# First layer of the last six units as seven block products, with the order from unit 5's second half on written anew

## The chip, the cores and the metric

One NeuronCore of a Trainium2 chip runs the kernel. The metric is device time in microseconds: the median of three runs of the kernel before is 290.37 us (290.33 to 292.88). In the profile PE is TensorE's matmuls, PEld its weight loads, DVE VectorE, ACT ScalarE, POOL GpSimd, SP the engine that issues most DMAs.

## What is computed

Attention in which a query sees only the keys of its own hash bucket (six sign bits of a projection), then a layer norm and a two-layer MLP with a residual.

```python
q_bits = (np.einsum('bhsd,dk->bhsk', q, proj) > 0)        # q, k, v: 4 x 8 x 768 x 64
k_bits = (np.einsum('bhsd,dk->bhsk', k, proj) > 0)        # bucket = the six bits as a number
scores = np.where(q_bucket == k_bucket, 0.125 * q @ k.T, -1e9)
attn = softmax(scores) @ v
x = attn.transpose(0, 2, 1, 3).reshape(4, 768, 512)
xn = (x - mu) / np.sqrt(var + 1e-06) * g_ln
out = x + np.maximum(xn @ w_ch1, 0.0) @ w_ch2             # 512 -> 2048 -> 512
```

## The kernel before

The work is cut into 12 units: unit u holds 256 of the 768 tokens of batch u // 3. Batches 0 to 3 are loaded, transposed and cast one after the other while earlier units compute. In a unit the eight heads form two groups g of four.

The program is one list of words, ORDER, in which each word is a function of the kernel, an engine (t TensorE, v VectorE, a ScalarE, p GpSimd, s SyncE) and its numbers. Each engine carries out its own words in the list's order; waits between engines come from the tiles that they share. Which buffer of a pool a tile gets is also written out, as one digit per tile in SLOTS.

The words of a unit, in the order of the data:

- `S.t.u.g.k` (L591): scores of 128 keys against 256 queries, four heads at once on four row strips: twelve matmuls of 256 columns. They go into tiles of the PSUM pool pp, three buffers of two banks.
- `E.a` (L608): the exp of one such tile, 128x1024, on ScalarE, into one of 15 SBUF buffers of pool E.
- `A.t` (L619): eight matmuls of 65 columns (v and a column of ones) into the accumulator acc, which also lives in pp.
- `na`, `nb`, `nc`, `ag`, `rs`, `ce` (L631 to L687): the accumulator is read, divided by its row sum, its mean and variance are taken, and the centred rows xc are written in bf16. `fl` (L690) is a DMA that writes them transposed into xnT.
- `F.t.u.p` (L710): the first layer, eight chunks p of 256 hidden columns: two blocks of 128, each of four matmuls over the 512 inputs, 256 token columns each, into one bank of the PSUM pool f, which has two. `R` (L718 on ScalarE, L720 on VectorE) reads a chunk once, with the relu, into hb.
- `ss` (L850), `P.t.u.1` to `P.t.u.7` (L865), `Y` (L870): the second layer by seven block products instead of eight (Winograd's form of Strassen's scheme). ss makes the block sums of hb, each P is eight matmuls of 256 columns into a bank of f, and Y adds the product to x. `O` (L882, L884) stores the unit.

So pool f carries the chunks F, the products P and a few small tiles, and pp carries the scores and acc. On TensorE the words S, A, F and P of neighbouring units stand mixed: at any time unit u's scores, unit u - 1's chunks or unit u - 2's products.

The functions `W1s`, `w1s`, `bs`, `M_`, `V_`, `U_`, `Q_`, `ru` (a first layer by seven products) stand in the code before too, but no word of the list before calls them, and WIDE is empty.

Of the kernel before, what the change touches and what calls it, by code (L numbers as in the profile page):

```python
# [64 lines left out]
A.t.4.0.0.2 F.t.2.0 A.t.4.0.1.0 A.t.4.0.1.1 na.v.4.0 F.t.2.4 E.a.4.1.0.0 E.a.4.1.0.2 R.a.2.0 R.v.2.4 ss.v.2.1  # L65
tu.v.2.1.0.1 S.t.5.0.0 N.a.5.0.0 S.t.5.0.1 E.a.5.0.0.1 S.t.5.0.2 P.t.2.2 Y.v.2.2 E.a.5.0.0.0 E.a.5.0.0.2
nb.v.4.0 fl.s.3.1 F.t.3.6 R.v.3.6 ss.v.2.2 P.t.2.1 Y.v.2.1 cv.v.2.0.2 S.t.4.1.3 S.t.4.1.4 N.a.4.1.1 S.t.4.1.5
mr.s.2.0.1 P.t.2.5 P.t.2.6 E.a.4.1.1.1 E.a.4.1.1.2 ss.v.2.4 Y.v.2.5 tu.v.2.1.0.0 A.t.4.1.0.2 P.t.2.3
E.a.4.1.1.0 nc.v.4.0 Y.v.2.6 A.t.4.1.1.2 Y.v.2.3 O.s.1.3 LX.s.3.0.1 LX.s.3.1.0 LX.s.3.1.1 mr.s.2.0.0
A.t.4.1.1.0 A.t.4.1.0.1 A.t.4.1.1.1 tu.v.2.1.1.0 ss.v.2.3 A.t.4.1.0.0 na.v.4.1 nb.v.4.1 LX.s.3.0.0 mr.s.2.0.2  # L70
F.t.3.3 nc.v.4.1 ag.v.4.0 P.t.2.7 S.t.5.0.3 R.a.3.3 N.a.5.0.1 S.t.5.0.4 S.t.5.0.5 ag.v.4.1 E.a.5.0.1.2 Y.v.2.7
E.a.5.0.1.1 CA.v.2.1.1 E.a.5.0.1.0 hm.t.2.1 bt.v.2.1 P.t.2.4 rs.p.4 Y.v.2.4 ce.v.4.0 F.t.3.4 S.t.5.1.0
tu.v.3.0.1.1 tu.v.3.0.1.3 CA.v.2.1.0 S.t.5.1.1 N.a.5.1.0 ce.v.4.1 R.a.3.4 S.t.5.1.2 su.v.2.0 E.a.5.1.0.1
F.t.3.0 mw.s.2.1 F.t.3.7 mr.s.2.0.3 O.s.1.0 A.t.5.0.0.0 tu.v.3.0.1.0 A.t.5.0.1.2 A.t.5.0.0.1 A.t.5.0.0.2
tu.v.3.0.1.2 R.a.3.0 F.t.3.2 mr.s.2.1.3 cv.a.2.0.0 R.a.3.7 E.a.5.1.0.0 R.a.3.2 A.t.5.0.1.0 A.t.5.0.1.1
tu.v.3.0.0.3 E.a.5.1.0.2 O.s.2.2 lv.s.2.4.2 na.v.5.0 O.s.2.0 tu.v.3.0.0.1 F.t.3.5 R.a.3.5 fl.s.4.1 F.t.3.1
R.v.3.1 mr.s.2.1.0 S.t.5.1.3 N.a.5.1.1 S.t.5.1.4 E.a.5.1.1.1 S.t.5.1.5 E.a.5.1.1.2 nb.v.5.0 P.t.3.2 ss.v.3.1
Y.v.3.2 P.t.3.1 P.t.3.5 S.t.6.0.0 E.a.5.1.1.0 CA.v.3.0.1 N.a.6.0.0 mr.s.2.1.1 lv.s.3.0.2 S.t.6.0.1 S.t.6.0.2
E.a.6.0.0.0 E.a.6.0.0.2 ss.v.3.2 Y.v.3.1 ss.v.3.4 Y.v.3.5 P.t.3.6 P.t.3.3 ss.v.3.3 nc.v.5.0 A.t.5.1.0.1
A.t.5.1.0.2 tu.v.3.0.0.2 A.t.5.1.0.0 Y.v.3.6 A.t.5.1.1.0 A.t.5.1.1.2 A.t.5.1.1.1 mr.s.2.1.2 na.v.5.1  # L80
E.a.6.0.0.1 fl.s.4.0 lv.s.2.4.3 P.t.3.7 tu.v.3.0.0.0 Y.v.3.3 nb.v.5.1 O.s.2.3 S.t.6.0.3 N.a.6.0.1 S.t.6.0.4
S.t.6.0.5 CA.a.3.0.0 Y.v.3.7 hm.t.3.0 bt.v.3.0 P.t.3.4 Y.v.3.4 lv.s.3.0.3 F.t.4.6 E.a.6.0.1.0 O.s.2.1
E.a.6.0.1.2 E.a.6.0.1.1 lv.s.3.0.1 nc.v.5.1 ag.v.5.1 ag.v.5.0 R.a.4.6 F.t.4.0 S.t.6.1.0 S.t.6.1.1 N.a.6.1.0
rs.p.5 S.t.6.1.2 R.v.4.0 ce.v.5.0 cv.a.2.4.2 F.t.4.7 E.a.6.1.0.0 cv.v.2.4.0 F.t.4.4 R.a.4.7 ce.v.5.1 on.p.2
fl.s.5.0 A.t.6.0.1.0 A.t.6.0.0.2 tu.v.3.1.0.1 E.a.6.1.0.1 E.a.6.1.0.2 A.t.6.0.1.2 lv.s.3.0.0 R.v.4.4 sp.t.2.0
# [36 lines left out]
R.v.8.7 rs.p.9 ce.v.9.0 A.t.10.0.0.0 A.t.10.0.0.2 A.t.10.0.1.2 A.t.10.0.1.1 F.t.8.5 R.a.8.5 ce.v.9.1 Y.v.7.4
F.t.8.0 O.s.7.2 na.v.10.0 R.v.8.0 S.t.10.1.3 fl.s.9.1 S.t.10.1.4 N.a.10.1.1 S.t.10.1.5 O.s.7.0 E.a.10.1.1.1
E.a.10.1.1.2 E.a.10.1.1.0 F.t.8.2 nb.v.10.0 R.v.8.2 F.t.8.3 R.a.8.3 F.t.8.4 R.v.8.4 S.t.11.0.0 N.a.11.0.0
S.t.11.0.1 S.t.11.0.2 F.t.8.1 E.a.11.0.0.0 R.v.8.1 P.t.8.2 O.s.7.3 Y.v.8.2 ss.v.8.1 E.a.11.0.0.2 fl.s.9.0
A.t.10.1.1.0 P.t.8.1 A.t.10.1.0.2 F.t.9.5 Y.v.8.1 A.t.10.1.1.2 A.t.10.1.0.1 A.t.10.1.0.0 A.t.10.1.1.1 ss.v.8.2
ss.v.8.4 R.a.9.5 E.a.11.0.0.1 P.t.8.6 na.v.10.1 nb.v.10.1 P.t.8.5 Y.v.8.5 S.t.11.0.3 ss.v.8.3 Y.v.8.6
# [19 lines left out]

TYPES = "222222333333333333333333"

WIDE = {}  # L150
SUMS = 12

SLOTS = dict(
# [15 lines left out]
    vnat="01010101",  # L169
    vsB="0101",  # L170
    vsum="000",
    x="012301230123",
    xnT="010101010101",
)

@with_exitstack
def kernel(
# [15 lines left out]
    nc = tc.nc  # L193
# [595 lines left out]
    def hq(u, t, i, h):  # L789
        return hb(u)[:, 8 * i + 4 * h : 8 * i + 4 * h + 4, P * t : P * t + P]  # L790
# [138 lines left out]
```

## Time and profile before

| | us |
|---|---|
| median of 3 runs | 290.37 |
| the profiled execution's own time | 290.62 |
| its span, first to last instruction | 288.7 |
| PE busy | 280.6 |
| DVE busy | 223.9 |
| ACT busy | 201.4 |
| POOL busy | 27.8 |

Busy time is the union of an engine's instructions. A matmul is listed with its full length from entry to result, so neighbours overlap, and what a stream of them costs is read from starts, or from a run of many. Group lines give line, engine, operation, tile, shape and count, then busy time and the mean length of one, then the engine's idle time ahead of them and what ended it. Timeline lines give the start, the length, and in brackets the idle time before.

### The profile page before, as it was taken

The numbers are of one execution on the slowest core, as the hardware profiler recorded it, in microseconds if no ns is written. First come the engines' busy times: TensorE is split into PE (matmuls) and PEld (weight loads), VectorE is DVE, ScalarE is ACT, GpSimd is POOL, SyncE is SP. The second block draws the span as 40 slices with busy tenths as digits, with TensorE's granted clock in tenths as the row PEclk, the third lists the DMA queues.
The fourth block names the chain that finished last, engine by engine and source line by source line (L and its number), as shares of the span: only waits on it lengthen the run. The fifth ranks groups of instructions, "written<-read, shape, count | busy, mean of one in ns | idle before, by whom it ended". The sixth has DMA issues, their size and how long they took to land.

```text
span 288.7 us, 10444 instructions
## 1 busy us (share of the span) xinstructions
PE 280.6 (97%) x4588; PEld 226.8 (79%) x4591; DVE 223.9 (78%) x507; ACT 201.4 (70%) x230; POOL 27.8 (10%) x65
## 2 busy tenths in 40 slices
PE   8999899999999999999999999999999999999994
PEld 4777777558886886887888878888888788898883
DVE  5767899899998998987896687794878486683553
ACT  4889999998786657869767686868685747714140
POOL 4560400110001002001001001000101001010000
PEclk9999999999999999999999999999999999999999
DMA  6999999156912985530710411500040500202162
GB/s 215 366 279 275 211 278 190 54 176 158 319 77 79 171 302 171 138 117 3 186 24 3 102 57 49 114 3 22 2 93 2 111 0 3 39 2 57 26 178 73
DMA packets 31056, 34.11 MB, mean 118 GB/s; under 512 B 15521, under 2 KB 27809, under 8 KB 31010
## 3 DMA queue, kind: packets, MB, share of 16 engines
q1 hardware_dynamic: 25938, 28.72, 34.7%
q0 software_dynamic: 4224, 4.19, 8.8%
q8 instruction: 36, 0.59, 0.8%
q10 hardware_dynamic: 848, 0.53, 0.7%
q14 instruction: 10, 0.08, 0.1%
HBM read 27.86 MB, written 6.88 MB: 120 GB/s over the span
## 4 chain that ended last, share of the span: by engine, by line
PE 92%; DVE 5%; ACT 1%; issue 1%; DVEq 0%; ACTq 0%
PE f L710 29%; PE sc L591 17%; PE X L865 13%; PE acc L619 12%; PE Yb L865 7%; PE Ya L865 3%; PE hp L535 3%; PE hf L403 3%; PE f L813 2%; PE warm L373 1%; DVE T L314 1%; ACT E L608 1%; DVE y L631 1%; DVE st L665 0%; DVE hb L720 0%
## 5 line engine op out<-in xcount | busy, mean ns | idle before, releaser
L608 ACT ACTIVATE E<-sc,bias_sb 128x1024 bf16<-128x1024 f32 x144 | 152.6, 1114 | 38.5 <-PE sc L591 36.8
L710 PE MATMUL f<-xnT,w_sb 128*128 128x256 bf16 x768 | 93.2, 273 | 0.6 <-ACT hb L718 0.2
L710 PEld LDWEIGHTS <-w_sb 128*128 128x128 bf16 x768 | 72.2, 98 | 13.5 <-issue 5.2
L718 ACT ACTIVATE hb<-f 128x512 bf16<-128x512 f32 x60 | 35.6, 598 | 31.8 <-PE f L710 27.7
L591 PE MATMUL sc<-qb,kb 32*128 32x256 bf16 x1152 | 51.4, 267 | 0.0
L591 PE MATMUL sc<-G 6*128 6x256 bf16 (+1 forms) x576 | 42.4, 271 | 0.8 <-ACT E L608 0.8
L619 PE MATMUL acc<-vaug,E 128*128 128x65 bf16 x1152 | 41.5, 193 | 0.2 <-ACT E L608 0.2
L619 PEld LDWEIGHTS <-E 128*128 128x128 bf16 x1152 | 40.1, 97 | 1.9 <-issue 0.6
L865 PEld LDWEIGHTS <-hb 128*128 128x128 bf16 x352 | 33.2, 98 | 7.2 <-issue 3.4
L720 DVE TENSOR_SCALAR hb<-f 128x512 bf16<-128x512 f32 x36 | 24.6, 687 | 16.5 <-PE f L710 16.0
L591 PEld LDWEIGHTS <-kb 32*128 32x128 bf16 x1152 | 30.5, 93 | 1.3
L591 PEld LDWEIGHTS <-G 6*128 6x128 bf16 (+1 forms) x576 | 17.2, 91 | 14.3 <-issue 12.0
L865 PEld LDWEIGHTS <-S 128*128 128x128 bf16 x264 | 24.8, 98 | 4.3 <-issue 1.3
L314 DVE STREAM_TRANSPOSE T<-X 128x384 f32<-128x384 f32 (+2 forms) x52 | 26.1, 536 | 0.0
L631 DVE SCALAR_TENSOR_TENSOR y<-vsB,acc 128x520 f32<-128x520 f32 x24 | 16.5, 689 | 9.8 <-PE acc L619 9.6
L870 DVE TENSOR_TENSOR x<-X,x 128x256 f32<-128x256 f32 x44 | 18.1, 413 | 7.4 <-PE X L865 7.1
L684 POOL TENSOR_SCALAR rs<-mv 128x2 f32<-128x2 f32 x12 | 2.8, 235 | 209.7 <-DVE mv L668 209.6
L865 PE MATMUL Yb<-w_sb,S 128*128 128x256 bf16 x176 | 22.9, 273 | 0.0
L865 PE MATMUL X<-wt,hb 128*128 128x256 bf16 x168 | 21.8, 273 | 0.0
L665 DVE BATCH_NORM_STATS2 st<-x 128x6 f32<-128x256 f32 x48 | 17.6, 412 | 0.3
L641 DVE TENSOR_TENSOR x<-y,rc 128x512 f32<-128x512 f32 x24 | 16.6, 692 | 0.8
L674 DVE TENSOR_SCALAR xc<-x,mv,rs 128x512 bf16<-128x512 f32 x22 | 11.4, 540 | 2.6 <-POOL rs L687 2.5
(94 smaller groups left out, 251.7 us busy)
## 6 DMA issues: line engine op xcount, KB each, us to landing
out_dram<-x SPq DMA_DIRECT2D x45, 128.0 KB
X<-in_k_dram SPq DMA_DIRECT2D x7, 768.0 KB
vn<-in_v_dram SPq DMA_DIRECT2D x24, 192.0 KB
X<-in_q_dram SPq DMA_DIRECT2D x6, 768.0 KB
w_sb<-in_moe_w_ch_dram POOLq DMA_DIRECT2D x8, 512.0 KB, 12.2
vn<-in_v_dram SPq DMA_DIRECT2D x2, 768.0 KB
X<-in_q_dram SPq DMA_DIRECT2D x2, 512.0 KB
Bd<-B SPq DMA_DIRECT2D x6, 96.0 KB
```

Of the source, the lines that this page charges most:

```text
L314: nc.vector.transpose(d[:, j], s[:, j, kj0 : kj0 + n])
L591: m = nc.tensor.matmul(sc(u, g, a, p)[:, bank, 256 * half : 256 * half + 256], lh, rh, start=(rep == 0), stop=(rep == 2), skip_group_check ...
L608: nc.scalar.activation(Ep(u, g, a, p), sc(u, g, a, p), AF.Exp, scale=EXP_SCALE, bias=bias_sb)
L619: nc.tensor.matmul(acc[:, qt, (D + 1) * i : (D + 1) * (i + 1)], Ep(u, g, a, p)[:, bank, 256 * half + P * qt : 256 * half + P * qt + P], va ...
L631: nc.vector.scalar_tensor_tensor(yt(u, g), vs, EPS_ROW, made[f"acc{u}_{g}"][:, :, :A], op0=AOP.mult, op1=AOP.add,)
L641: nc.vector.tensor_tensor(xo, a[:, :, :, 0:D], rc.to_broadcast([P, 2, 4, D]), op=AOP.mult)
L665: nc.vector.bn_stats(stats(u)[:, qt, g], xt(u)[:, qt, 256 * g : 256 * g + 256])
L710: nc.tensor.matmul(f1[:, n].rearrange("p (t x) -> p t x", t=2), w1_sb[:, dt, P * nt : P * nt + P], xnT(u)[:, :, dt], start=(dt == 0), stop ...
L718: nc.scalar.activation(hb(u)[:, 2 * p : 2 * p + 2], f1, AF.Relu)
L720: eng.tensor_scalar_max(hb(u)[:, 2 * p : 2 * p + 2], f1, 0.0)
L865: nc.tensor.matmul(f2, lh[:, n], rh[:, n], start=(first and n == 0), stop=(n == 7), skip_group_check=True)
L870: nc.vector.tensor_tensor(x, made[f"{prod(u, k)}{u}"], x, op=AOP.add)
```

## The change

In units 6 to 11 the words F and R are gone. Their first layer is done by seven products of blocks, with W1 cut in 2 x 2 blocks (256 inputs x 1024 hidden) and xnT in 2 x 2 blocks (256 inputs x 128 tokens):

- `w1s` (eight instructions in all, 128x1024 bf16, on VectorE) makes four sums of blocks of W1 once, in the order's stretch of units 5 to 7; they stay in two buffers of E and two of X, so that X and E have fewer buffers for the rest.
- `bs` (four a unit, 128x256 bf16, VectorE) makes sums of blocks of xnT.
- `M.t.u.p.h`: product p for half h of the hidden columns: four blocks of 128 hidden columns, each two matmuls of 128 token columns, eight matmuls in all. Products 1, 6, 7 and 4 accumulate in this order in a bank `Ma`, 5 and 3 in `Me`, 2 in `Mb`.
- `V` copies Ma or Me as it stands at that time (after 1, after 6, after 5) to SBUF in fp32; `U` adds such a copy to Mb, Me or Ma and writes hb; `Q` is the relu of the finished Ma into hb; `ru` takes the relu of what U wrote, 128x1024 in place.

On an accumulator Ma the order is product 1, V, product 6, V, product 7, U, product 4, Q, each waiting for the one ahead of it. In units 6 to 8 all three tiles are in pool f. In units 9 to 11 (WIDE) Ma and Me each take a tile of pp, of which one bank is used.

The list is the same up to the middle of unit 4's weighted sums (500 words); from there on all is new. Counted over the rest, VectorE loses 24 R and two casts and gets 10 V, 36 U, 3 Q, 16 ru, 24 bs and 8 w1s; ScalarE loses 24 R and gets 26 V, 9 Q, 2 ru and two casts. One load of batch 3 (queries of the second head group) stands later on SyncE, behind stores of units 1 and 2.

VectorE while unit 7's first layer is on TensorE, before. Names: f1_7p is unit 7's chunk p, y and x the attention's rows, hb7 the operand of its second layer, xc8 the centred rows of unit 8.

```order
L720 TENSOR_SCALAR hb7_4468<-f1_70_4769 128x512
L668 BN_AGGR mv8_4797<-st8_4499 128x2 x2
L720 TENSOR_SCALAR hb7_4468<-f1_74_4707 128x512
L720 TENSOR_SCALAR hb7_4468<-f1_77_4833 128x512
L674 TENSOR_SCALAR xc8_4852<-x8_4365,mv8_4797,rs8_4828 128x512 x2
L720 TENSOR_SCALAR hb7_4468<-f1_73_4843 128x512
L720 TENSOR_SCALAR hb7_4468<-f1_71_4857 128x512
L638 RECIPROCAL rc90_4923<-y90_4779 128x8
```

The same place now. Ma70 is accumulator Ma of unit 7, half 0; V711 the copy of product 1, half 1.

```order
L805 TENSOR_TENSOR hb7_4825<-Me70_4847,V760_4827 128x4x128
L811 TENSOR_SCALAR hb7_4825<-Ma70_4766 128x4x128
L798 COPY V711_4945<-Ma71_4936 128x512
L805 TENSOR_TENSOR hb7_4825<-Mb71_4947,V711_4945 128x4x128
L687 TENSOR_SCALAR xc8_4979<-x8_4536,mv8_4803,rs8_4859 128x512
L819 TENSOR_SCALAR hb7_4825<-hb7_4825 128x8x128
L687 TENSOR_SCALAR xc8_4979<-x8_4536,mv8_4803,rs8_4859 128x512
L798 COPY V751_5033<-Me71_4984 128x512
L805 TENSOR_TENSOR hb7_4825<-Ma71_4936,V751_5033 128x4x128
L805 TENSOR_TENSOR hb7_4825<-Me71_4984,V761_4993 128x4x128
L651 RECIPROCAL rc90_5080<-y90_4845 128x8
```

Where VectorE read independent chunks, it now reads the same two accumulators again and again, with unit 8's xc and a ru between two of those reads.

ScalarE at that place, before: exps of unit 9's second head group, and then unit 10's.

```order
L718 ACTIVATE hb7_4468<-f1_76_4629 128x512
L608 ACTIVATE E9_101_4678<-sc9_101_4653,bias_sb_66 128x1024
L608 ACTIVATE E9_102_4741<-sc9_102_4664,bias_sb_66 128x1024
L608 ACTIVATE E9_100_4743<-sc9_100_4650,bias_sb_66 128x1024
L608 ACTIVATE E9_111_4812<-sc9_111_4784,bias_sb_66 128x1024
```

ScalarE there now:

```order
L621 ACTIVATE E9_101_4720<-sc9_101_4668,bias_sb_66 128x1024
L796 COPY V710_4814<-Ma70_4766 128x512
L796 COPY V760_4827<-Ma70_4766 128x512
L796 COPY V750_4857<-Me70_4847 128x512
L621 ACTIVATE E9_111_4899<-sc9_111_4873,bias_sb_66 128x1024
L621 ACTIVATE E9_110_4932<-sc9_110_4870,bias_sb_66 128x1024
L621 ACTIVATE E9_112_4934<-sc9_112_4886,bias_sb_66 128x1024
L796 COPY V761_4993<-Ma71_4936 128x512
```

Three copies in a row stand between two exps, and the fourth behind three exps.

On TensorE the words of unit 7's first layer were eight F, mixed with A and S of units 9 and 10; now they are fourteen M, mixed with the same A and S. The core of the diff, with two lines of the list (the whole list and the buffer digits differ from there on):

```diff
-A.t.4.0.0.2 F.t.2.0 A.t.4.0.1.0 A.t.4.0.1.1 na.v.4.0 F.t.2.4 E.a.4.1.0.0 E.a.4.1.0.2 R.a.2.0 R.v.2.4 ss.v.2.1
...
+A.t.9.0.0.1 M.t.7.2.0 ag.v.8.1 bs.v.7.2 A.t.9.0.0.2 V.a.7.1.0 M.t.7.6.0 bs.v.7.4 U.v.7.1.0 V.a.7.6.0
+A.t.9.0.0.0 A.t.9.0.1.1 na.v.9.0 M.t.7.5.0 ag.v.8.0 V.a.7.5.0 rs.p.8 M.t.7.7.0 S.t.9.1.3 N.a.9.1.1 O.s.6.0
...
-WIDE = {}
+WIDE = {9,10,11}
...
     def Mt(u, name):
         if u in WIDE and name[1] in "ae":
-            both = ps(f"Mae{name[2:]}", [P, 2, 512], "pp")
-            made[name] = both[:, "ae".index(name[1])].rearrange("p (n x) -> p n x", x=P)
-            return made[name]
+            return ps(name, [P, 2, 512], "pp")[:, 0].rearrange("p (n x) -> p n x", x=P)
         return ps(name, [P, 4, P], "f")
...
     def V_(eng, u, p, h):
-        src = made[f"M{'e' if p == 5 else 'a'}{u}{h}"]
+        src = Mt(u, f"M{'e' if p == 5 else 'a'}{u}{h}")
...
     def U_(eng, u, c, h):
         src, other, t, i = {1: ("b", 1, 0, 0), 2: ("e", 6, 1, 0), 4: ("a", 5, 1, 1)}[c]
-        nc.vector.tensor_tensor(hq(u, t, i, h), made[f"M{src}{u}{h}"], made[f"V{u}{other}{h}"], op=AOP.add)
+        nc.vector.tensor_tensor(hq(u, t, i, h), Mt(u, f"M{src}{u}{h}"), made[f"V{u}{other}{h}"], op=AOP.add)
...
     def Q_(eng, u, h):
         if eng is nc.scalar:
-            nc.scalar.activation(hq(u, 0, 1, h), made[f"Ma{u}{h}"], AF.Relu)
+            nc.scalar.activation(hq(u, 0, 1, h), Mt(u, f"Ma{u}{h}"), AF.Relu)
```

The function that the new words call for a product, as it stands before and after:

```python
    def M_(eng, u, p, h):
...
        name = f"M{'_abeaeaa'[p]}{u}{h}"
        first = name not in made
        m = Mt(u, name)
        for n in range(4):
            nt = 4 * h + n
            for kt in range(2):
                nc.tensor.matmul(
                    m[:, n], lh(kt)[:, P * nt : P * nt + P], rh[:, kt],
                    start=(first and n == 0 and kt == 0), stop=(kt == 1), skip_group_check=True,
                )
```

More of the change, by code (lines that the diff above doesn't have):

```diff
@@ L69 @@
[L69 to L73, printed above, removed]
@@ L124 @@
[L124 to L127, printed above, removed]
-N.a.11.0.1 S.t.11.0.4 O.s.7.1 S.t.11.0.5 E.a.11.0.1.0 E.a.11.0.1.2 P.t.8.3 P.t.8.7 Y.v.8.3 F.t.9.0 Y.v.8.7
@@ L171 @@
     vsum="000",
-    x="012301230123",
+    x="012301230213",
     xnT="010101010101",
```

170 lines of the change are left out of this document (96 added, 74 removed).

## The prediction

> **What bounds the kernel now.** I read the core's span and clock first, then engine totals and the chain of waits, then long windows, then the groups and the timeline for prices.
>
> ```profile
> core 0: 288.7 us, clock 1.000
> PE 280.6 (97%) x4588; PEld 226.8 (79%) x4591; DVE 223.9 (78%) x507; ACT 201.4 (70%) x230; POOL 27.8 (10%) x65
> PE 92%; DVE 5%; ACT 1%; issue 1%; DVEq 0%; ACTq 0%
> ```
>
> The clock is full and 92% of the chain that ended last is PE: the order of work on TensorE is the time. The windows tell how much room the other engines have. Their columns are window, length, then busy time (and count) of PE, PEld, DVE, ACT and POOL.
>
> ```profile
> 60.00:120.00 60.00, 59.95 (x956) 47.40 (x956) 56.65 (x121) 45.51 (x53) 3.60 (x6) 1.00 0.62 178
> 120.00:180.00 60.00, 59.99 (x1029) 48.90 (x1027) 48.45 (x106) 43.97 (x49) 3.34 (x10) 1.00 0.26 71
> 180.00:288.70 108.70, 104.38 (x1553) 89.74 (x1550) 71.29 (x155) 59.84 (x71) 3.71 (x8) 1.00 0.20 48
> ```
>
> From 60 us until the last 4 us PE has no idle time. In 60 to 120 us DVE is busy for 56.65 of 60 us beside it, so this kind of order can keep PE full with DVE at 94%. After 180 us DVE has 37 us and ACT 49 us free. That is where the change adds their work: the drain of unit 8's first half, beside which unit 6's products will stand, is at 181.84.
>
> ```profile
> 181.84 0.69 DVE L631 SCALAR_TENSOR_TENSOR y<-vsB,acc 128x520 f32<-128x520 f32 x1
> ```
>
> **PE: removed and added.** Removed are 48 F chunks of eight matmuls of 256 columns. In the tail they run with nothing in between:
>
> ```profile
> 272.08 6.28 PE L710 MATMUL f<-xnT,w_sb 128*128 128x256 bf16 x56
> 273.16 0.60 ACT L718 ACTIVATE hb<-f 128x512 bf16<-128x512 f32 x1 [4.65 <-PE f L710]
> 274.03 0.60 ACT L718 ACTIVATE hb<-f 128x512 bf16<-128x512 f32 x1 [0.28 <-PE f L710]
> 277.52 0.60 ACT L718 ACTIVATE hb<-f 128x512 bf16<-128x512 f32 x1 [0.27 <-PE f L710]
> 278.20 1.04 PE L865 MATMUL Ya<-w_sb,hb 128*128 128x256 bf16 x8
> ```
>
> A chunk ends every 0.873 us (274.03 to 277.52 is four of them), so a matmul with its weight load takes 0.109 us, and 48 chunks 41.9 us. Added are 84 products (six units, two halves, seven each) of eight matmuls of 128 columns, 672 pairs. The one place that has such pairs is the first unit's transposes:
>
> ```profile
> L695 PE MATMUL ft<-ident,xc x8: 216/218/230, 29.4 to 30.0; 128*128 128x128 bf16 x8
> 29.85 0.38 PE L695 MATMUL ft<-ident,xc 128*128 128x128 bf16 x4
> 252.06 1.47 PE acc L619 x48
> 241.18 1.10 PE sc L591 x36
> ```
>
> Four of them take 0.38 us, of which the last one's own 0.22 is no spacing: 0.16 over three steps, 0.053 to 0.056 us each. Half of a 256-column matmul is 0.0546. I take 0.0555: 37.3 us, a saving of 4.6 us. Bounds: 0.0546 gives 5.2 us. On the other side, the weight load is not what limits a pair: accumulating products with 65 columns and the same 128x128 weights go at 1.47/48 = 0.031 us. The exps' scores (36 in 1.10 us) and those products do not change in number.
>
> A rule speaks against this price. The Trainium skill, "TensorE: Matmul & The Clock Gate", section "Back-to-back issue gap", gives about 81 ns per matmul of 128 columns for a sustained stream of weight load and matmul pairs. By it the 672 would take 54.4 us, 12.5 more than the chunks removed, and the sum would be about 303. The eight pairs of this trace, 0.056 apart at most, disagree, but they are only bursts of four.
>
> **DVE and ACT: what lies beside.** Prices:
>
> ```profile
> L608 ACT ACTIVATE E<-sc,bias_sb 128x1024 bf16<-128x1024 f32 x144 | 152.6, 1114 | 38.5 <-PE sc L591 36.8 <-DVE S L850 1.1 <-ACT E L608 0.3
> L718 ACT ACTIVATE hb<-f 128x512 bf16<-128x512 f32 x60 | 35.6, 598 | 31.8 <-PE f L710 27.7 <-PE sc L591 3.9
> L720 DVE TENSOR_SCALAR hb<-f 128x512 bf16<-128x512 f32 x19 | 12.9, 686 | 14.3 <-PE f L710 14.2
> L641 DVE TENSOR_TENSOR x<-y,rc 128x512 f32<-128x512 f32 x8 | 5.5, 692 | 0.3
> L850 DVE TENSOR_TENSOR S<-hb 128x1024 bf16<-128x1024 bf16 x10 | 6.9, 687 | 0.6 <-ACT hb L718 0.3
> L850 DVE TENSOR_TENSOR S<-hb 128x512 bf16<-128x512 bf16 x2 | 0.8, 424 | 4.6 <-ACT hb L718 4.6
> L464 DVE TENSOR_SCALAR w_sb<-w_sb,gT 128x512 bf16<-128x512 bf16 x12 | 3.4, 346 | 0.0
> 267.59 0.68 DVE L850 TENSOR_TENSOR hb<-hb 128x1024 bf16<-128x1024 bf16 x1
> 268.18 0.68 DVE L850 TENSOR_TENSOR S<-hb,S 128x1024 bf16<-128x1024 bf16 x1
> ```
>
> After unit 5 the order has on DVE: 10 copies V, 36 sums U and 3 Q, all 128x512 out of PSUM, at 0.69 each 33.8 us; 24 block sums bs of 256 columns, 0.28 each by the line through 0.42 (512) and 0.69 (1024), 6.7 us; 16 relus ru over 128x1024 bf16. No row is a ru: L464 is half as wide at 0.35, so a ru is 0.35 to 0.69; I take 0.5, 8.0 us. Gone are 19 R, 13.0 us. Together 71.3 + 35.5 = 106.8 us where PE wants about 104. But the two rows at 267.59 and 268.18 start 0.59 apart at 0.68 each: an instruction whose successor is ready costs 0.09 less. If half of the 224 instructions of the stretch are packed so, the load is 97 us of about 106, 91%. That is under the 94% of 60 to 120 us, with little to spare.
>
> The Trainium skill, "VectorE: DVE Perf Modes", section "Mode 4×_2P — both tricks at once", lets a one-source bf16 instruction in SBUF do four elements a cycle. By that a ru would be about 0.42 us (an estimate: 0.27 streaming, the rest fixed), and the sum 1.3 us smaller; no run here shows it.
>
> ACT gets 26 V and 9 Q at 0.60 (20.9 us), two ru priced at an exp's 1.11 as ceiling, and loses 27 R (16.1): 59.8 + 7.0 = 67 of 106 us. It is no bound.
>
> **Ahead of that,** DVE gets the eight 1024-wide weight sums w1s, 8 x 0.69 = 5.5 us, and loses 5 R (3.4 us). DVE idles 11.5 of 60 us in 120 to 180, which hides it: 0, and up to 5.5 if that cover is gone. One of batch 3's four loads of q and k is queued later on SP, behind unit 2's stores; its transposes on DVE wait for it, 0 to 3 us. I take 0.
>
> **New waits.** A first-layer chunk had one read; an accumulator of the products is read four times in a row (V, V, U, Q), and each next product on it waits for the read. A step is: eight starts and the last one's length, 7 x 0.055 + 0.22 = 0.61; 0.04 until the reader starts (the chunk begun at 272.08 ends at 273.12, ACT starts at 273.16); 0.60 to 0.69 for the read; at most 0.08 back to PE (278.12 to 278.20). That is 1.38 us, 5.5 for a half, 11.0 for the two halves of units 6 to 8, which share the two f banks. Between a unit's first product and the first P, which reads Q, PE has in its order: 14 products at 0.445 (6.2), A words of eight at 0.245, S words of twelve at 0.37. Unit 6: 12 A and 6 S, 11.3 us. Unit 7: 11 and 6, 11.2. Unit 8: 11 and 9, 12.2. Slack is 0.3, 0.2 and 1.2 us, so what stands ahead of a read on DVE or ACT (xc's 0.54, the v sums, an exp of 1.11) goes on the path. Following the rows by hand with these durations I find four late reads in unit 6, 0.05 to 0.2 each, together 0.6, and 0.45 in unit 7; unit 8 0.3. In units 9 to 11 the halves have pp banks of their own and overlap: 5.5 us of chain beside 10.9 to 12.3 us of PE work. By hand unit 11 shows no wait; for DVE's queue I put 0.4 each on 9 and 10. Sum 2.1 us, bounds 0 and 7.5 (below).
>
> **Sum** against the profiled execution's own 290.6 us (span 288.7 and 1.9 around it): 290.6 - 4.6 + 2.1 = 288.1. The median of the runs is 0.25 lower, so 288.0 with rounding. The tail behind the last PE instruction (4 us of adds and stores) is unchanged.
>
> **Rivals.**
> 1. Everything is covered: saving 4.6 to 5.2, no wait; 285.3 to 286.6. For it: PE full beside DVE at 94% in 60 to 120 us. Against: slack of 0.2 to 0.3 us in units 6 and 7.
> 2. The reads bind, slower than before. Place: the f banks of units 6 to 8, 24 serial reads in the queues of a DVE that is 91% loaded and an ACT with exps of 1.11. If each is late by half a DVE instruction, 0.35 us, that is 8.4 - 1.7 slack + 0.8 in units 9 to 11 = 7.5 us: 293.3. It decides from 0.23 us per read, (4.6 + 1.7 - 0.8)/24, where the saving is gone.
> 3. The weight load shows in a long stream of 128-column pairs. A load lasts 0.098 us in the trace; a pair halfway between 0.055 and that is 0.077: 51.7 us, 9.8 more than the chunks, 300. This is the skill rule's case above; against it stand the 0.031 us pairs.
>
> ```profile
> L619 PEld LDWEIGHTS <-E 128*128 128x128 bf16 x1152 | 40.1, 97 | 1.9 <-issue 0.6
> ```
>
> 4. The stretch before unit 6 pays: the late load or the weight sums cost 3 us; 291.
>
> **Chances.** Forecast (286.7 to 290.4) 0.45; rival 1 0.18; rival 2 (290.4 to 297) 0.25; rival 3 0.04; rival 4 0.08. The range 285.5 to 294.0 leaves out the upper third of rival 2, rival 3 and the lowest edge of rival 1, under 0.2. The forecast's own range is 286.7 to 290.4. About 1%, 2.9 us, is what a measurement tells from no change: under 287.5 lie rival 1 and a third of the forecast, 0.33; over 293.3 half of rival 2, rival 3 and a little of rival 4, 0.22; within, 0.45.
>
> **What would show it.** PE: the new product line should have starts 0.055 apart, its 672 matmuls some 37 us busy; if over 44, rival 3. PE idle "until DVE or ACT" at the product line after 180 us should sum to about 2 us, most of it in units 6 and 7; 5 or more, named DVE U, V or Q, is rival 2; none is rival 1. DVE busy from unit 6 on should be 93 to 100 us. Idle PE before 180 us, or DVE waiting for X, is rival 4. The forecast is wrong if the median is outside 286.7 to 290.4.

## The result, and the profile after

The changed kernel takes 289.57 us, median of 20 runs (289.13 to 290.31), the kernel before on the same chip 290.87 us (20 runs, 290.04 to 292.88); the ratio is 0.9956, 95% interval 0.9945 to 0.9967. A second set of runs gave 289.44 against 290.41 us, 0.9966 (0.9954 to 0.9978). So the change wins 1.0 to 1.3 us, 40 to 55% of the 2.4 us that the prediction gave it: the direction was right, the size was not.

The span with its clock, the engines' totals and the shares of the chain of waits, of the kernel after:

```profile
core 0: 287.9 us, clock 1.000
PE 280.2 (97%) x4879; PEld 227.4 (79%) x4879; DVE 252.0 (88%) x578; ACT 211.7 (74%) x245; POOL 30.0 (10%) x65
PE 86%; DVE 9%; ACT 2%; issue 1%; POOLq 0%; POOL 0%; DVEq 0%; ACTq 0%
```

The same three windows as before (PE, PEld, DVE, ACT, POOL):

```profile
60.00:120.00 60.00, 59.95 (x956) 47.31 (x955) 55.84 (x118) 46.75 (x55) 3.24 (x8) 1.00 0.59 169
120.00:180.00 60.00, 60.00 (x1051) 48.35 (x1049) 52.53 (x117) 46.45 (x54) 5.04 (x8) 1.00 0.35 83
180.00:287.90 107.90, 103.83 (x1823) 90.94 (x1819) 95.60 (x217) 66.44 (x81) 4.78 (x8) 1.00 0.20 48
```

PE is still full until the last 4 us, with DVE at 95.6 and ACT at 66.4 us in the last window (the prediction worked out 97 and 67). A full PE is no proof of useful work here: the profile models the ends of matmuls, so a short gap between two starts shows as busy. The loss is found only in the distances between starts.

For that, two marks that all kernels of this study have: the first score word of unit 5 (S.5.0.0) and the fourth score word of unit 11's second group (S.11.1.3). Up to the second mark units 6 to 9 have done their first layer, behind it come units 10 and 11. This table (us, starts from the PE timeline; the end is the last matmul's start) takes the loading at the start of the program out, whose length alone varies by 1.0 us between the profiled executions (S.5.0.0 at 97.4 to 98.4 us, in one of them at 99.7):

| kernel | S.5.0.0 | S.11.1.3 | last PE start | first part | last part | both |
|---|---|---|---|---|---|---|
| before | 97.75 | 249.03 | 284.20 | 151.28 | 35.17 | 186.45 |
| after | 97.83 | 249.93 | 283.77 | 152.10 | 33.84 | 185.94 |

In the last part the products bring 1.33 us. Worked out: 16 chunks at 0.873 us are 13.97 us, 28 product words of eight pairs at 0.056 us are 12.54 us, 1.4 us less. In the first part, where 2.8 us should be won (32 chunks, 27.9 us, for 56 words, 25.1 us), the kernel got 0.82 us longer. So 3.6 us were lost there. Behind the last PE start the changed kernel is 0.4 us shorter here (287.9 - 283.77 = 4.1 us against 288.7 - 284.20 = 4.5); in its second profile (after_again) that end takes 4.3 us, and over all kernels of the study 4.1 to 4.8, so this is no part of the effect.

**Where they went.** PE rows of the kernel before around one group of scores:

```profile
176.23 1.04 PE L865 MATMUL Yb<-w_sb,S 128*128 128x256 bf16 x8
177.20 0.29 PE L591 MATMUL sc<-G 6*128 6x256 bf16 x4
...
177.54 0.28 PE L591 MATMUL sc<-G 6*128 6x256 bf16 x4
...
177.88 0.28 PE L591 MATMUL sc<-G 6*128 6x256 bf16 x4
...
178.31 1.05 PE L865 MATMUL X<-wt,hb 128*128 128x256 bf16 x8
```

A P word of eight at 0.109 us begun at 176.23 would let the next word start at 177.10; the scores (four matmuls at a time, each on its own strip of the array's rows) start at 177.20, 0.10 us late. Score words follow one another every 0.34 us, so P could follow at 178.22; it starts at 178.31, 0.09 us late. Entering and leaving a run of score words thus costs 0.19 us together, and over the 28 runs behind S.5.0.0's own the median is 0.192. The kernel before has its score words in runs of three. The changed kernel cuts eight of these runs, to place single score words between products:

```profile
183.44 0.61 PE L787 MATMUL Ma<-bs,w_sb 128*128 128x128 bf16 x8
183.98 0.29 PE L604 MATMUL sc<-G 6*128 6x256 bf16 x4
184.10 0.39 PE L604 MATMUL sc<-qb,kb 32*128 32x256 bf16 x8
184.43 0.62 PE L787 MATMUL Ma<-xnT,w_sb 128*128 128x128 bf16 x8
184.88 0.61 PE L787 MATMUL Mb<-xnT,w_sb 128*128 128x128 bf16 x8
185.43 0.61 PE L604 MATMUL sc<-G 6*128 6x256 bf16 x4
185.76 0.49 PE L604 MATMUL sc<-qb,kb 32*128 32x256 bf16 x8
186.19 0.62 PE L787 MATMUL Ma<-bs,Wx 128*128 128x128 bf16 x8
```

Two things are to be seen. A product word takes 0.45 us from start to start (184.43 to 184.88, 0.056 a pair), but 0.55 in front of a score word. And the single word S.9.0.0 at 185.43 has 0.61 in place of 0.29 us on its first four matmuls: it stands ahead of its group, and two of its four row strips start 0.33 us after the others, when the first of two exps, which ran on ScalarE from 184.59 to 185.70, has left their bank. Behind S.5.0.0's own run there are 36 runs of score words. Their excess over 0.336 us a word sums to 8.03 us against 5.37 before: 8 x 0.195 = 1.56 us for the ends of the added runs, and 1.1 us of such waits inside the runs, 0.7 of it at three single words (S.9.0.0, S.10.0.0, S.11.0.0). Waits outside score words (distances above the usual spacing, summed) are 1.9 us against 0.9: 1.0 us more. Together: -4.3 + 2.66 + 1.0 = -0.6 us; the table has -0.51.

### The profile page after: what moved, and what is told of

It is laid out like the page before. It is cut to its first block, busy times and chain, and to the rows that moved or that the text cites. A ratio compares the mean times of both kernels' runs of the same rounds, so it can differ in the third digit from the quotient of the medians.

```text
span 287.9 us, 11150 instructions
## 1 busy us (share of the span) xinstructions
PE 280.2 (97%) x4879; PEld 227.4 (79%) x4879; DVE 252.0 (88%) x578; ACT 211.7 (74%) x245; POOL 30.0 (10%) x65
## 4 chain that ended last, share of the span: by engine, by line
PE 86%; DVE 9%; ACT 2%; issue 1%; POOLq 0%; POOL 0%; DVEq 0%; ACTq 0%
PE sc L604 17%; PE f L723 14%; PE X L876 12%; PE acc L632 11%; PE Ma L787 6%; PE Yb L876 6%; PE Me L787 3%; PE hp L548 3%; PE Ya L876 3%; PE hf L416 3%; PE f L824 2%; ACT E L621 2%; PE Mb L787 1%; PE warm L386 1%; DVE T L327 1%
## 5 line engine op out<-in xcount | busy, mean ns | idle before, releaser
L604 PE MATMUL sc<-qb,kb 32*128 32x256 bf16 x1152 | 52.5, 267 | 0.0
L723 PE MATMUL f<-xnT,w_sb 128*128 128x256 bf16 x384 | 47.0, 273 | 0.5 <-ACT hb L731 0.2
L604 PE MATMUL sc<-G 6*128 6x256 bf16 (+1 forms) x576 | 43.3, 272 | 0.9 <-ACT E L621 0.8
L723 PEld LDWEIGHTS <-w_sb 128*128 128x128 bf16 x384 | 35.7, 98 | 8.3 <-issue 4.2
L604 PEld LDWEIGHTS <-G 6*128 6x128 bf16 (+1 forms) x576 | 17.8, 91 | 15.6 <-issue 11.4
L731 ACT ACTIVATE hb<-f 128x512 bf16<-128x512 f32 x36 | 21.3, 599 | 8.5 <-PE sc L604 5.5
L327 DVE STREAM_TRANSPOSE T<-X 128x384 f32<-128x384 f32 (+2 forms) x52 | 26.3, 539 | 0.0
L697 POOL TENSOR_SCALAR rs<-mv 128x2 f32<-128x2 f32 x12 | 3.8, 315 | 207.9 <-DVE mv L681 207.8
L787 PEld LDWEIGHTS <-w_sb 128*128 128x128 bf16 x288 | 17.2, 98 | 1.5 <-issue 1.1
L787 PEld LDWEIGHTS <-Wx 128*128 128x128 bf16 x288 | 16.9, 98 | 1.6 <-issue 1.5
```

Source lines behind the costliest of these rows:

```text
L327: nc.vector.transpose(d[:, j], s[:, j, kj0 : kj0 + n])
L604: m = nc.tensor.matmul(sc(u, g, a, p)[:, bank, 256 * half : 256 * half + 256], lh, rh, start=(rep == 0), stop=(rep == 2), skip_group_check ...
L723: nc.tensor.matmul(f1[:, n].rearrange("p (t x) -> p t x", t=2), w1_sb[:, dt, P * nt : P * nt + P], xnT(u)[:, :, dt], start=(dt == 0), stop ...
L731: nc.scalar.activation(hb(u)[:, 2 * p : 2 * p + 2], f1, AF.Relu)
L787: nc.tensor.matmul(m[:, n], lh(kt)[:, P * nt : P * nt + P], rh[:, kt], start=(first and n == 0 and kt == 0), stop=(kt == 1), skip_group_ch ...
```

## Experiments

Two theories. **Switch theory**: the saving was spent on the ends of the added runs of score words. My first price for it, 0.27 us a run, put the way out at 0.17 us; against the score words' own spacing it is 0.10. **Reads theory**: the saving was lost to late reads of the accumulators and the load of VectorE and ScalarE, and single score words cost nothing. Where an edit moves words, the numbers of banks and slots follow and are not shown.

The same table for all experiments (us), with the ratio of the runs to those of the kernel before:

| kernel | first part | last part | both | median | ratio (interval) |
|---|---|---|---|---|---|
| before_split8 | 154.07 | 35.17 | 189.24 | 293.42 | 1.0075 (1.0052 to 1.0099) |
| before_split16 | 156.46 | 35.17 | 191.63 | 295.80 | 1.0160 (1.0136 to 1.0184) |
| before_split8_last | 153.96 | 35.17 | 189.13 | 293.44 | 1.0089 (1.0072 to 1.0106) |
| after_grouped | 155.06 | 33.85 | 188.91 | 293.04 | 1.0057 (1.0035 to 1.0080) |
| no_copies | 151.75 | 33.85 | 185.60 | 289.44 | 0.9948 (0.9924 to 0.9972) |
| grouped_no_copies | 154.38 | 33.84 | 188.22 | 292.26 | 1.0044 (1.0018 to 1.0071) |
| no_reads | 151.72 | 33.84 | 185.56 | 289.46 | 0.9964 (0.9949 to 0.9979) |
| grouped_no_reads | 152.03 | 33.84 | 185.87 | 289.64 | 0.9961 (0.9937 to 0.9985) |
| first_four | 152.08 | 37.04 | 189.12 | 293.25 | 1.0074 (1.0047 to 1.0102) |
| last_two | 152.44 | 36.46 | 188.90 | 293.31 | 1.0079 (1.0052 to 1.0106) |
| last_two_b | 151.51 | 35.07 | 186.58 | 290.02 | 0.9980 (0.9961 to 0.9999) |
| last_two_c | 151.20 | 33.85 | 185.05 | 288.70 | 0.9947 (0.9929 to 0.9966) |
| late_only | 161.78 | 33.84 | 195.62 | 299.52 | 1.0288 (1.0255 to 1.0321) |
| last_three | 157.29 | 35.11 | 192.40 | 295.82 | 1.0190 (1.0163 to 1.0217) |

### Cuts alone, without any product

Eight runs of the kernel before cut, two of them here:

```diff
-P.t.5.3 S.t.8.1.0 N.a.8.1.0 ... S.t.8.1.1
+S.t.8.1.0 P.t.5.3 N.a.8.1.0 ... S.t.8.1.1
...
-S.t.8.1.4 E.a.8.1.1.1 S.t.8.1.5 R.v.6.5 F.t.6.6
+S.t.8.1.4 E.a.8.1.1.1 R.v.6.5 F.t.6.6 S.t.8.1.5
```

> The kernel before with eight of its runs of three score words cut in two, one word of a whole-array kind (F or P) between the parts, at the eight places where the changed kernel cuts them (8.1 twice, 9.0, 9.1, 10.0, 10.1, 11.0 twice); no product of 128 columns in it, no read of an accumulator added. Switch theory (each further run of score words costs what the trace shows at its two ends: about 0.096 us going in, 0.17 us coming out, 0.27 us in all): 8 x 0.27 = 2.2 us more, a ratio of 1.007 to the kernel before. Reads theory (the gain was lost to late reads of the accumulators and to VectorE's load; cutting the runs is free): a ratio of 1.000, within 0.001.

> The same with sixteen runs cut, from unit 6's second half on. Switch theory: 16 x 0.27 = 4.3 us more, a ratio of 1.015, and twice the step of the kernel with eight. Reads theory: 1.000, within 0.002. If a score bank were late at some of the cuts, the idle time of TensorE ahead of the score line grows; the pitch at the ends of the runs tells that apart.

Measured: 293.42 - 291.02 = 2.4 us for eight cuts, 4.8 us for sixteen, 0.30 us a cut both times (in the table 2.8 and 5.2 us, 0.35 and 0.32 a cut). The reads theory gives 0 here: that single score words cost nothing is refuted. PE rows of the kernel with eight:

```profile
175.07 1.04 PE L865 MATMUL X<-wt,hb 128*128 128x256 bf16 x8
176.04 0.39 PE L591 MATMUL sc<-G 6*128 6x256 bf16 x4
176.16 0.49 PE L591 MATMUL sc<-qb,kb 32*128 32x256 bf16 x8
176.59 1.05 PE L865 MATMUL Yb<-w_sb,S 128*128 128x256 bf16 x8
177.57 0.29 PE L591 MATMUL sc<-G 6*128 6x256 bf16 x4
```

One score word between two P words takes 0.55 us (176.04 to 176.59) against 0.34 inside a run, 0.10 of the excess being a wait for a bank (0.39 in place of 0.29 us). The size agreed with 0.27 a run, but not for its reason: the ends cost 0.20 at such a place, and the word that was brought ahead of its group waits for banks (up to 0.3 us in units 9 to 11). So a third kernel cuts only in front of a run's last word, where no bank has to come free earlier.

```diff
-S.t.11.0.4 O.s.7.1 S.t.11.0.5 E.a.11.0.1.0 E.a.11.0.1.2 P.t.8.3
+S.t.11.0.4 O.s.7.1 P.t.8.3 S.t.11.0.5 E.a.11.0.1.0 E.a.11.0.1.2
```

> The kernel before with eight runs of score words (6.1, 7.0, 7.1, 8.0, 8.1, 9.1, 10.1, 11.0, the second half of each group) cut in front of their last word, one P or F word between; no score word stands earlier than before. If a cut costs 0.20 us at the ends of the runs and the rest of the 0.30 us was banks not yet free: 8 x 0.20 = 1.6 us more, ratio 1.005 to 1.006. If every cut costs 0.30 us: 2.4 us more, ratio 1.008, as in the first run with eight cuts. Reads theory: 1.000.

Measured: 2.6 us, 0.33 a cut; the expectation of 1.6 us was too low. Its rows show the clean price at the cut:

```profile
227.50 0.39 PE L591 MATMUL sc<-qb,kb 32*128 32x256 bf16 x8
227.82 1.05 PE L710 MATMUL f<-xnT,w_sb 128*128 128x256 bf16 x8
228.81 0.29 PE L591 MATMUL sc<-G 6*128 6x256 bf16 x4
228.93 0.39 PE L591 MATMUL sc<-qb,kb 32*128 32x256 bf16 x8
229.25 1.92 PE L710 MATMUL f<-xnT,w_sb 128*128 128x256 bf16 x16
```

The lone word takes 0.44 us (228.81 to 229.25) and the chunk ahead of it 0.99 in place of 0.87: about 0.2 us beyond their own spacing (0.20 to 0.21 at each of the eight cuts). The other 1.1 us is spread: 0.34 at a P word that now comes a word earlier than its input, 0.1 at each of five later groups and 0.3 at a sixth, where strips of the first word wait as at 185.43 above; the delayed words' exps, and with them the banks, come later. So a cut costs 0.2 us at its ends at every place tried, and here as much as 0.13 us more because the order around it was fitted to uncut runs.

### The runs put together again

```diff
-S.t.8.1.4 CA.a.3.1.1 S.t.8.1.3 ... M.t.6.3.0 ... N.a.8.1.1 E.a.8.1.1.1 M.t.6.4.0 S.t.8.1.5
+S.t.8.1.3 N.a.8.1.1 S.t.8.1.4 S.t.8.1.5 CA.a.3.1.1 ... M.t.6.3.0 ... E.a.8.1.1.1 M.t.6.4.0
```

> The changed kernel with the eight cut runs of score words put together again (from 37 runs to 29); the products between them now stand in rows of up to six. Switch theory: 8 x 0.27 = 2.2 us less for the ends of the runs, less what the products then wait where a score word had covered a read: at most about 0.3 us at each of the eight places, so 287.4 to 289.6 us, ratio 0.989 to 0.997 to the kernel before. Reads theory: the score words were free cover, so each place now shows a copy or sum of 0.6 to 0.7 us less one product of 0.45 us and more: 2 to 4 us slower than the changed kernel, 291.6 to 293.6 us.

Measured: 293.04 us, in the table 3.0 us more than the changed kernel (3.5 between the medians of two sets of runs, in which the kernel before differs by 0.15 us as well). Here the switch theory alone misses and the reads theory is right. PE, DVE and ACT in the kernel with the runs together:

```profile
184.26 0.62 PE L787 MATMUL Me<-xnT,Wv 128*128 128x128 bf16 x8
184.71 0.61 PE L787 MATMUL Ma<-bs,w_sb 128*128 128x128 bf16 x8
```

```profile
184.91 0.69 DVE L805 TENSOR_TENSOR hb<-Me,V 128x512 bf16<-128x512 f32 x1 [0.46 <-PE Me L787]
185.17 3.11 ACT L621 ACTIVATE E<-sc,bias_sb 128x1024 bf16<-128x1024 f32 x3
185.52 0.68 DVE L811 TENSOR_SCALAR hb<-Ma 128x512 bf16<-128x512 f32 x1
185.66 0.61 PE L787 MATMUL Ma<-xnT,w_sb 128*128 128x128 bf16 x8 [0.34 <-DVE hb L805]
```

The product at 184.71 is the last on the first half's Ma; with it both f banks are full. The second half's first product needs the bank of Me, which the sum at 184.91 reads until 185.60: PE starts at 185.66, 0.50 us after it could. In the changed kernel the score word at 183.98 stands at just this place. The window 180 to 240 us, first of the changed kernel, then of this one:

```profile
180.00:240.00 60.00, 59.88 (x1180) 50.21 (x1177) 54.41 (x120) 47.78 (x53) 1.85 (x4) 1.00 0.19 41
```

```profile
180.00:240.00 60.00, 56.93 (x1146) 49.11 (x1145) 51.85 (x111) 45.88 (x51) 1.86 (x4) 1.00 0.18 40
```

PE idles 3.1 us where it idled 0.1. So both theories hold a part: the score words between the products are cover for the reads, and their price is the ends of the runs. Beside the products of units 6 to 8 the cut runs cost 2.7 us and save more.

### Which reads

Copies left out: `V` words dropped, and in U_

```diff
-        nc.vector.tensor_tensor(hq(u, t, i, h), Mt(u, f"M{src}{u}{h}"), made[f"V{u}{other}{h}"], op=AOP.add)
+        nc.vector.tensor_scalar_max(hq(u, t, i, h), Mt(u, f"M{src}{u}{h}"), 0.0)
```

> The changed kernel without the copies V of the accumulators and with U as a relu of the accumulator alone (the first addend of each sum is left out), everything else in the same order: 30 us less on ScalarE and VectorE, and no product waits until a copy has read its bank. Switch theory: the products' waits on reads are about 1.4 us in all, of which the copies' part goes: 288.2 to 289.0 us. Reads theory: most of the 4 us that the saving lost comes back: 285.5 to 286.5 us.

> The changed kernel with the eight cut runs of score words put together, and without the copies V, U as a relu of the accumulator alone (the first addend of each sum is left out). The run with the runs put together alone was 3.5 us slower than the changed kernel: the cut score words had been cover. If they were cover for the copies of the accumulators, products no longer wait here and putting the runs together shows its own worth: 2.2 us less than without copies alone, 287.2 to 288.0 us, ratio 0.987 to 0.990. If they covered the sums' and relus' reads as well (U, Q), about half of the 5.7 us stays: 290 to 291.5 us.

Measured: 289.44 us, more than either theory expected and nothing against the changed kernel (the table has 0.3 us less), though 22 us of copies are gone (36 copies at 0.59 and 0.69 us; the 30 us of the expectation were too many). And with the runs together 292.26, again above both expectations: the copies were not what the score words cover. Only 0.7 of the 3 us go (188.91 to 188.22). The next pair takes the reads from the banks and leaves the work:

```diff
+    def acc(u, name, h):
+        return Mt(u, name) if u in WIDE else xnT(u)[:, h]
...
-            nc.scalar.activation(hq(u, 0, 1, h), Mt(u, f"Ma{u}{h}"), AF.Relu)
+            nc.scalar.activation(hq(u, 0, 1, h), acc(u, f"Ma{u}{h}", h), AF.Relu)
```

(and so in V_, U_ and Q_ on both engines).

> The changed kernel, in its own order, but in units 6 to 8 the copies, sums and relus take their first operand from the unit's transposed input in SBUF in place of the accumulator (so units 6 to 8 get another first layer). The same instructions stand on VectorE and ScalarE, only no bank waits for a read. Switch theory: the products' waits on reads in units 6 to 8 are 0.5 us in the trace, and only they go: 289.0 to 289.3 us, ratio 0.994 to 0.995. Reads theory: the larger part of the 4 us that the saving lost comes back: 286.5 to 287.5 us, ratio 0.985 to 0.988.

> The same with the eight cut runs of score words put together again. Without a read to wait for, the products need no score word as cover. Switch theory: 2.2 us less than without reads; of the waits that putting together brought (5.4 us: 3.4 at products, 2.0 at the accumulations, at P and at the scores behind exps) the 3.4 us go and the 2.0 us stay: 288.6 to 289.4 us, and 3.6 to 4.4 us less than the kernel with the runs put together and the reads kept (293.0 us). If the waits there were not for the reads of the accumulators, it stays at 292 to 293 us.

Measured: 289.46 us, in the table 0.4 us less than the changed kernel. That is all that the reads of units 6 to 8 cost it; the reads theory's 2 to 3 us are not there. With the runs together 289.64 us (a little above the 288.6 to 289.4 expected), in the table 3.0 us less than the same order with its reads; the copies were 0.7 of that, so most of those waits were reads of U and Q. Against the cut order without reads it wins nothing (the table has 0.3 us more), since the other waits that putting together brought stay: 0.57 us at a P word, 0.4 us at each of three accumulations behind products (0.05 to 0.11 with the runs cut), 0.4 us at a score word, 2.0 us together. The ends saved are 1.4 us, and the waits for banks inside the runs do not shrink: the second word of group 9.0 (PE timeline, 188.03) comes 0.95 us late behind an exp. So this pair shows that the reads were what the cut words cover; what the ends alone are worth in the changed kernel it does not show.

### One part alone

The first try joined the kernel before, up to S.11.1.3, with the changed kernel behind it; first_four is the other half.

> The kernel before, in its own order, up to the second half of unit 11's second score group; from there the changed kernel's order. So F stands in units 0 to 9 and products in units 10 and 11 alone (28 words of products, none near a score word), and the combinations of the weights are made in units 8 to 11. Switch theory: no run of score words is cut, and the changed kernel was 1.33 us shorter than the one before from this point to its end, so that is the gain: 289.2 to 289.7 us, ratio 0.995 to 0.996, as much as the whole change gives. Reads theory: each product word pays alike, wherever it stands; a third of the words brings a third of the change's gain, 0.4 us, ratio 0.998 to 0.999.

> The other part alone: the changed kernel's order up to that point, then the order of the kernel before. Products in units 6 to 9 (56 words), F in 10 and 11. Switch theory: this stretch holds the eight cut runs of score words (2.2 us) and nearly all waits of the products on reads (1.4 us) against 2.8 us saved, so nothing is won: 290.6 to 291.8 us, ratio 1.000 to 1.004. Reads theory: two thirds of the change's gain, 0.9 us, ratio 0.996 to 0.998.

Both came out slower than either parent, 293.31 and 293.25 us. In first_four the first part agrees (152.08 us, as in the changed kernel), but the last part has a P word 1.04 us late and a chunk 0.69 us late, which neither parent has: joints of my own. In last_two the tile for unit 10's block sums lay in the slot of unit 11's last exp, which the accumulations read until 254.93; the profile names a copy V as the releaser, but that had ended at 254.50:

```profile
253.31 1.62 PE L632 MATMUL acc<-vaug,E 128*128 128x65 bf16 x48
253.91 0.59 ACT L796 COPY V<-Ma 128x512 f32<-128x512 f32 x1
...
255.03 0.29 DVE L765 TENSOR_TENSOR bs<-xnT 128x256 bf16<-128x256 bf16 x1 [1.71 <-ACT V L796]
...
256.19 0.51 PE L787 MATMUL Ma<-bs,Wx 128*128 128x128 bf16 x6 [0.80 <-DVE bs L765]
```

As totals these two runs decide nothing on the theories. The second try:

```diff
-S.t.8.0.0 w1s.v.1.1 ... S.t.8.1.0 w1s.v.1.0
+Y.v.5.4 w1s.v.1.1 ... R.v.6.5 w1s.v.1.0
...
-F.t.9.1 fl.s.10.0 fl.s.10.1
+ce.v.10.1 fl.s.10.1 ce.v.10.0 fl.s.10.0
```

> Products in units 10 and 11 alone once more; the first try lost 3 us to waits of its own making: the tile of the input's combinations lay in a slot that a score's exp had just left, and the weights' combinations stood ahead of sums that P waits for. Here those combinations stand behind the last sum of a unit, the transposes of unit 10 are issued right behind its normalization, and tiles of the last stretch take the slot that has been free longest. Switch theory, as before: 289.2 to 290.0 us, ratio 0.995 to 0.998. Reads theory: 290.2 us or more, ratio 0.998 and above.

290.02 us, at the edge of both expectations, with two waits left that the changed kernel doesn't have there, of 0.40 us at a product and this one, a P word behind another's bank:

```profile
276.97 1.04 PE L876 MATMUL X<-wt,hb 128*128 128x256 bf16 x8
278.68 0.49 PE L876 MATMUL Ya<-w_sb,hb 128*128 128x256 bf16 x3 [0.67 <-DVE x L881]
```

X and Ya lay in the same bank one behind the other. The third try gives the small PSUM tiles behind S.11.1.3 the banks that they have in the changed kernel, and nothing else:

> Products in units 10 and 11 alone, as in last_two_b, with the small PSUM tiles of the last stretch in the banks that they have in the changed kernel. Switch theory: the waits of 0.40 us (products) and 0.83 us (P) in that stretch go, the stretch from unit 11's last scores to the end takes 33.8 us as in the changed kernel against 35.2 us in the one before: 288.7 to 289.4 us, ratio 0.993 to 0.996, as short as the changed kernel or shorter, with a third of its products. Reads theory: 290.0 us again, ratio 0.998.

> The changed kernel itself, for the comparison with last_two_c on the same chip: 289.6 us, ratio 0.995 to 0.996 to the kernel before, by both theories.

Measured: 288.70 us (8 runs, 288.31 to 290.67) against 289.44 us of the changed kernel on the same chip (7 runs, 289.16 to 289.86); seven of the eight are below the lowest of the changed kernel. (The profiled one is the 290.67. Its S.5.0.0 comes 1.9 us later than in the changed kernel, most of it because the granted clock stood at 0.50 from 30.8 to 34.1 us; the table leaves that out.) First and last rows of the last part, before, after and this kernel:

```profile
249.03 0.29 PE L591 MATMUL sc<-G 6*128 6x256 bf16 x4
...
283.44 1.04 PE L865 MATMUL Yc<-wt,hb 128*128 128x256 bf16 x8
```

```profile
249.93 0.29 PE L604 MATMUL sc<-G 6*128 6x256 bf16 x4
...
283.01 1.04 PE L876 MATMUL Yc<-wt,hb 128*128 128x256 bf16 x8
```

```profile
250.92 0.29 PE L604 MATMUL sc<-G 6*128 6x256 bf16 x4
...
284.00 1.04 PE L876 MATMUL Yc<-wt,hb 128*128 128x256 bf16 x8
```

From score to last word 34.41, 33.08 and 33.08 us. Products in units 10 and 11 alone, a third of them, bring 1.7 us (1.4 in the table), more than the whole change: in units 6 to 9 the products cost more than they save once their cover is paid for, by 0.8 us in the first part of first_four and of the changed kernel itself.

> The changed kernel with F put back in units 6 to 8 at the places of their products, and the eight cut runs of score words put together, so products stand in units 9 to 11 alone, where their sums lie in the score banks. Switch theory: 42 words of products fewer (18.8 us) and 24 F chunks more (20.9 us) cost 2.1 us, eight switches fewer give back 2.2 us, and the waits in units 6 to 8 (about 0.9 us) go: 288.4 to 289.6 us, ratio 0.992 to 0.996; the order is not tuned for it, so a late score bank may cost some tenths. Reads theory: half of the words bring half of the gain: 290.2 us, ratio 0.998.

> Products in units 9 to 11, where the score banks take two of the three accumulators: the order of the kernel before to the end of unit 11's first score group (two P words moved behind that group, the two F chunks of unit 9 there taken out), then the changed kernel's order. No run of score words is cut. Switch theory: 24 F chunks become 42 words of products, 2.1 us less, and no switch is added: 288.6 to 289.6 us, ratio 0.992 to 0.996, the shortest of all if no new wait comes with the splice. Reads theory: half of the words, half of the gain: 290.2 us, ratio 0.998.

Both tries to have units 9 to 11 without cut runs failed, at 299.52 and 295.82 us. In late_only the chunks stand where products stood, on two f banks, and wait for their relus (up to 1.8 us); in last_three the words moved behind a score group were missing in front of it, and scores and accumulations wait for exps; about 2.6 us of its time went to a stretch at half the clock (last section). They say only that an order doesn't bear such swaps, and whether unit 9 alone pays stays open.

## Where the prediction held and where it failed

- **The price of a pair** held: 0.056 us in the median of 672 against 0.0555, a saving of 41.9 - 37.6 = 4.3 for 4.6 us. The rule of the Trainium skill, "TensorE: Matmul & The Clock Gate", section "Back-to-back issue gap", of about 81 ns for 128 columns is not borne out: also in streams of five words, 40 pairs, the distance stays at 56 ns. Rival 3 is out.
- **The step that failed** is one sentence: "The exps' scores (36 in 1.10 us) and those products do not change in number." The number did not change, the cost did. The rows of before had the price, 0.10 us into and 0.09 us out of each run of score words, and the order showed 36 runs for 28; I read neither. It measured 2.66 us: 1.56 at the ends of eight more runs, 1.1 in waits for banks inside the runs. With it the prediction's own sum would have been 290.6 - 4.6 + 2.1 + 2.7 = 290.8 us.
- **The waits** were sized 2.1 us and measured 1.0 us net of smaller waits elsewhere, about 1.2 us at the products themselves: in units 6 to 8 0.2 to 0.4 us each, 0.3 of it at accumulations behind products, in units 9 to 11 0.27 us at one product and 0.14 at a P word. Leaving the reads out won 0.4 us. The prediction counted the score words of that stretch into its slack of 0.2 to 1.2 us, so it had their cover right and their price not. The sign it named for them, idle PE at the product line, stayed empty (L787 shows no idle time until DVE or ACT), which it would have read as rival 1; the waits show only in the starts. That 289.57 us lies inside 286.7 to 290.4 is in part luck: the waits, priced too high, made up for part of the ends that were not priced (the 290.8 above, less the 0.25 us by which the median is lower, is outside).
- **Rival 2**, the reads bind (293.3 us), is a real mechanism that the order keeps away: with the runs together the kernel took 293.04 us. It was bought off for the 2.7 us above. (Rival 1's range was added up wrongly: savings of 4.6 to 5.2 us without a wait give 285.2 to 285.8, not up to 286.6 us; nothing rests on it.)
- **DVE and ACT** were right: 95.6 for 97 and 66.4 for 67 us in the last window. The prices stand in three groups of the kernel after:

```profile
L805 DVE TENSOR_TENSOR hb<-Ma,V 128x512 bf16<-128x512 f32 x12 | 8.3, 689 | 1.3 <-PE Ma L787 0.7 <-ACT V L796 0.4
L796 ACT COPY V<-Ma 128x512 f32<-128x512 f32 x17 | 9.8, 587 | 8.9 <-PE Ma L787 8.6
L819 DVE TENSOR_SCALAR hb<-hb 128x1024 bf16<-128x1024 bf16 x16 | 6.7, 422 | 0.2
```

  The relu ru took 0.422 us; I had taken 0.5, and the estimate from the Trainium skill, "VectorE: DVE Perf Modes", section "Mode 4×_2P — both tricks at once", was 0.42: the trace agrees.
- **Ahead of unit 6** nothing was lost: from S.5.0.0 to S.6.0.0 26.3 us before and 26.4 after, to S.8.0.0 70.3 and 69.8. Rival 4 is out. The end behind the last matmul, called unchanged, was 0.4 and 0.2 us shorter in the two profiles of the changed kernel, within what it varies by from kernel to kernel.

## What to carry to other kernels

When an order is remade, count not only the instructions of each kind but the places where PE goes from one kind to another, and price them from the distances between starts, not from busy time: a PE that reads 100% busy hid 2.7 us here. Work that is slipped in as cover has a price of its own; a saving is worth making first where no cover is needed, here in the last two units. And a reordered kernel is compared by marks in the program that both share, stretch by stretch, since joints, early loads and stretches at half the clock shift totals by as much as the effect.

## What was not expected of the hardware

Going from matmuls on all 128 rows to four at a time on strips of the rows, and back, cost 0.09 to 0.11 us each way, median 0.096, in every kernel of this study. Why is not shown.

In last_three PE stood idle for 1.9 us (240.0 to 241.9), with idle times of 0.9 and 0.5 us in the 7 us ahead; within that time, at 240.8, the granted clock fell (the column behind POOL):

```profile
232.00:240.00 8.00, 6.40 (x133) 4.87 (x131) 6.68 (x17) 4.12 (x5) 0.00 (x0) 1.00 0.02 3
240.00:242.00 2.00, 0.13 (x3) 0.14 (x4) 0.68 (x4) 2.00 (x3) 0.92 (x2) 0.69 0.00 0
242.00:246.00 4.00, 4.00 (x61) 4.00 (x60) 0.00 (x0) 1.44 (x3) 0.00 (x0) 0.50 0.00 0
246.00:250.00 4.00, 4.00 (x52) 3.72 (x50) 2.95 (x6) 0.78 (x2) 0.00 (x0) 0.80 0.08 17
```

It came back at 247.6. So PE worked at half the clock for 5.7 us, with the matmuls of products 0.107 us apart: 2.6 us lost by the starts, on top of the wait. A wait of 1.8 us in late_only, 1.6 of it idle, left the clock at 1.00:

```profile
208.00:211.00 3.00, 3.00 (x55) 2.37 (x53) 0.97 (x3) 2.16 (x3) 0.93 (x2) 1.00 0.02 7
211.00:214.00 3.00, 1.41 (x13) 0.98 (x11) 0.37 (x1) 2.05 (x3) 0.00 (x0) 1.00 0.00 0
214.00:218.00 4.00, 4.00 (x86) 3.42 (x85) 1.92 (x4) 2.85 (x4) 0.00 (x0) 1.00 0.18 37
```

Nor does it take a long idle time: in last_two_c the clock stood at 0.50 from 30.8 to 34.1 us after 7 us in which PE was idle for 0.9 us in all, none of it longer than 0.4. The same stretch of no_copies, idle for 0.9 us too, stayed at 1.00. What decides is not shown.
